# The middle channel block of a convolution, moved from VectorE to ScalarE and accumulating DMAs

## The chip, the cores and the metric

The program runs on one core of a Trainium2 chip. Its engines are TensorE (PE in the profile, its weight loads PEld), VectorE (DVE), ScalarE (ACT), GpSimd (POOL) and SyncE (SP). Each works through its own instructions in the order in which they were written, and waits on semaphores for the others. DMAs are issued from the queues of SP, of POOL and, rarely, of ACT. The metric is the device time of one execution in microseconds (us); less is better.

## The reference

A causal depthwise convolution over 7 positions, whose weights are the softmax of 8 rows (one row for each group of 24 channels), is followed by two matrix products with a gelu between them:

```
w = softmax(weight)                         # (8, 7), row h serves channels 24h .. 24h+23
a[b, s, d] = sum over k of w[h(d), k] * x[b, s - 6 + k, d]      # x is (8, 4096, 192), zeros ahead of it
h = a.reshape(32768, 192) @ w_in            # w_in (192, 2048)
g = h * sigmoid(1.702 * h)
out = g @ w_out                             # w_out (2048, 192), everything float32
```

## The kernel before

**Steps.** The tokens are worked in 32 steps, numbered 0 to 31 (`big` in the code), of 1024 tokens each: two sequences of 512 tokens, side by side. The 192 channels are three blocks of 64 (`c` = 0, 1, 2). One block of a step, with both sequences, is a 128 x 512 tile. The middle block is `c` = 1.

**Two products.** Both matrix products are computed by schemes that save multiplications at the price of additions. The first product of a step (`hidden`, L664, called for v = 0 and v = 1) is 21 terms for each v, each of two 64-row matmuls of 512 columns (`product1`, L611). Its inputs are the convolved blocks and eight sums of them (`SUMS_C`, on GpSimd from step 2 on). The second product (`second`, L973) follows `PLAN` (L926), an order written out by hand. It runs through 78 "go" items: one go is three main matmuls and one side matmul of 128 x 32 by 256 columns. I call the place after n gos "position n". Between the gos, PLAN puts sums of hidden blocks on VectorE (`sum`), accumulating DMAs from GpSimd's queue (`acc`), seeds (ScalarE copies that start an accumulation in PSUM), joins (VectorE additions of partial results) and transposes to the output. A side result is complete every four gos (every two between positions 36 and 42), and ScalarE then copies it out of PSUM (L1016, `act.copy(to, d)`), so that copies stand at positions 4, 8, ..., 36, 38, 40, 42, 46, 50, and so on.

**The blocks of `g`.** The hidden values lie in the tile `g`, in 16 blocks; with four rooms of other tiles they are named "spots" 0 to 20 (spots 5 to 20 are blocks of `g`). A spot has 128 x 1024 values, four quarters of 256. The second product consumes the spots one after the other, so some of them are free again before it is over.

**The convolution before the change.** The convolution of a step is made while earlier steps run, in three ways:

- Block 0: seven ScalarE multiplications (`tap`, L512, the instruction is on L516), one for each k. The first goes to the destination in `conv_t`, the other six to "homes", half-spots of spots 13, 16 and 15. Six accumulating DMAs of 256 KB then add them up in a tree, homes 1+2, 3+4, 5+6, then destination+1, 3+5, destination+3 (`TREE`, L509; `end_taps`, L527, the DMAs are on L530). The taps of step n+2 stand in PLAN of step n, at positions 50, 54, 58, 61, 65, 69 and 72.
- Block 1: one VectorE multiplication and six VectorE multiply-adds (`conv`, L497; L502 and L504), in the first product (v = 0) of the step ahead. `prepare` (L580) lists them, and `work` (L1049) hands them out against a budget of time.
- Block 2: seven ScalarE taps and six GpSimd additions (L518), in the first product (v = 0) of the step ahead, through `taps_at`.

`next_tap` (L1054) emits the next entry of the list `ready`; `need` (L1060) empties a list up to a label.

**What sets the order.** The order on each engine is that of the program text: PLAN in the second product, the calls in `hidden` in the first. The main loop's `begin` puts the preparation of step n+2 into the lists just ahead of the second product of step n.

**The places that matter below.** In PLAN, `("acc", 7, 10)` reads spot 10 and `("acc", 12, 9)` reads spot 9 by a 512 KB DMA; `("acc", 18, 14)` is the last one. At position 58 stand a side copy and then `("seed", "k5", "p2", 1)`, at 60 the join `("join", "p2", "p4", "+", "k3")`, which reads the PSUM region p4 and overwrites p2, whose old value the seed keeps, and at 62 `("main", 4, 6, "p4", 0)`, which accumulates into p4. `("main", 12, 18, "p3", 0)` at 70 reads spot 18.

Of the kernel before, what the change touches and what calls it, by code (L numbers as in the profile page):

```python
# [15 lines left out]
def kernel(  # L16
# [126 lines left out]
        flat = osbs[:, i * BLK : (i + 1) * BLK] if i < 2 else room[:, ROOMS[i - 2], :]  # L143
        return flat.rearrange("p (k t) -> p k t", k=NG)

    KEPT_LATE, TAP_SPOTS = 3, {0: (13, 16, 15), 2: (14, 17, 18), 3: (15, 16, 19)}

    def kept(i):

# [20 lines left out]
    def place(big, b):  # L170

        if b == V1:
            return V8 if big % 2 else C31
        return C31 if b == V8 and big % 2 else b
# [319 lines left out]
    def conv_src(big, c, k, ns=slice(0, 2)):  # L494
        return xts[big][:, c, ns, Q - PAD + k : Q - PAD + k + T]

    def conv(big, c, k, ns=slice(0, 2), times=vec.tensor_scalar_mul):  # L497
        src = conv_src(big, c, k, ns)
        dst = own(big)[:, 2 * c + ns.start : 2 * c + ns.stop, :]
        tap = cw[:, c, k : k + 1]  # L500
        if k == 0:
            times(dst, src, tap)  # L502
        else:
            vec.scalar_tensor_tensor(  # L504
                out=dst, in0=src, scalar=tap, in1=dst, op0=ALU.mult, op1=ALU.add
            )

    DMA_TAPS = (0,)
    TREE = {2: [(1, 2)], 4: [(3, 4)], 6: [(5, 6), (0, 1), (3, 5), (0, 3)]}  # L509
    PAIRS_1 = {2: [(1, 2)], 4: [(3, 4)], 6: [(5, 6)]}  # L510

    def tap(big, c, k):  # L512
# [3 lines left out]
        act.mul(home, conv_src(big, c, k), cw[:, c, k : k + 1])  # L516
        if k and c not in DMA_TAPS and big > 1:
            nc.gpsimd.tensor_add(dst, dst, home)  # L518
# [61 lines left out]
    def prepare(big):  # L580

        v1 = place(big, V1)
        def convs(*cs):
            for c in cs:
                for k in range(K):
                    yield "", 0.76 if k else 0.48, lambda c=c, k=k: conv(big, c, k)

        cost = 0.34 if big == 1 else 0.0
        yield from convs(1)
        yield f"conv {big}", 0.0, lambda: None  # L590
        if big == 1:
            dst = own(1)[:, 0:2, :]
            for k in (1, 3, 5):
                yield "", 0.7, lambda k=k: vec.tensor_add(dst, dst, tap_home(1, 0, k))
        yield f"done {big}", 0.0, lambda: need(f"taps {big}")
        yield "", cost, lambda: sums_c(big, 0)
        yield f"first {big}", 0.0, lambda: cross_when(True, big, v1, v1 + 1)
        yield "", 0.0, lambda: cross_when(False, big, 0, C31)
        for i in range(1, len(SUMS_C)):
            yield "", cost, lambda i=i: sums_c(big, i)  # L600
        rest = (C31, V8) if big % 2 else (C31 + 1, NB)
        yield f"all {big}", 0.0, lambda: cross_when(False, big, *rest)

    def prepare_taps(big):

        for c in (0, 2):
            for k in range(K):
                yield "", 1.0, lambda c=c, k=k: tap(big, c, k)
        yield f"taps {big}", 0.0, lambda: None
# [54 lines left out]
    def hidden(big, v, x, z, y, sums, work, fetch, last=lambda: None):  # L664

        def pe(slot, *ts, first=False):
            terms(big, v, slot, *ts, first=first)

        def taps_at(n):
            for _ in range(0 if v else n):
                next_tap()

        def early(i):
            for item in (EARLY_G if big > 1 else EARLY_G_1)[i] if v else ():
                sum_g(*item)


        if v:  # L680
            pe(z, 7, first=True)
            give(True, big)
        if v:
            pe(sums, 12)
            copy2(k15, sums)
            pe(x, 5, 17)
        else:
            pe(x, 5)
            pe(sums, 12)
            copy2(k15, sums)  # L690
            pe(x, 17)
            taps_at(1)
        gelu(B11, 0, v, x)
        if not v:
            pe(z, 7, first=True)
        pe(sums, 0)
        copy2(k16, sums)
        taps_at(2)
        last()
        def turn_next():  # L700
            if big + 2 < N_BIG:
                need(f"done {big + 1}")
                turn_x(big + 2)

        early(0)
        if not v:
            work(2.0 if big > 1 else 1.6)
        elif big == 1:
            work(3.2)

        pe(y, 6, 14, first=True)
        sum2(vec.tensor_sub, x, z, k15)
        early(1)
        if not v or big == 1:
            work(1.6 if big > 1 else 1.2)
        pe(sums, 13)
        copy2(k19, sums)
        pe(x, 2)
        copy2(k18, x)
        taps_at(2)  # L720
        pe(z, 11)
        pe(sums, 20, 10)
        sum2(vec.tensor_sub, k15, y, k19)
        gelu(B12, 0, v, sums)
        pe(x, 4)
        copy2(k20, x)
        sum2(vec.tensor_sub, k19, z, k19)
        early(2)
        if not v or big == 1:
            work(1.1)  # L730
        gelu(B22, 1, v, k19)
        gelu(B22, 0, v, k15)
        taps_at(2)
        pe(y, 8)
        pe(sums, 1, 9, first=True)
        pe(y, 15)
        if v and big == 1:
            turn_next()
        elif not v:
            work(2.2 if big > 1 else 1.1)  # L740
        sum2(vec.tensor_add, k20, k20, sums)
        sum2(vec.tensor_sub, k16, y, k16)
        gelu(B11, 1, v, k20)
        pe(x, 18)
        gelu(B21, 1, v, x)
        early(3)
        fetch()
        if not v:

            copy2(y, z)  # L750
        gelu(B21, 0, v, k16)
        if not v:
            work(1.2)
        if not v and big > 1:
            turn_next()
        pe(sums, 3, 19)
        if not v:
            work(0.7)
        sum2(vec.tensor_add, k18, k18, sums)
        return lambda: gelu(B12, 1, v, k18)  # L760
# [150 lines left out]
    def store(big, n, o=None, queues=(nc.sync,) * 3):  # L911
# [45 lines left out]
        ("turn", 1, 0, 0, "k6"), ("store", 0, 0), ("main", 24, 19, "p5", 0), ("go", 2), ("final",),  # L957
        ("join", "k1", "p3", "-", "k3"), ("go", 1), ("join", "k2", "p2", "-", "k4"),
        ("turn", 0, 0, 1, "k1"), ("store", 0, 1), ("go", 1), ("turn", 0, 1, 1, "k2"), ("store", 1, 1),
        ("join", "k1", "p5", "+", "k5"), ("turn", 0, 1, 0, "k1"), ("join", "k8", "k8", "+", "k0"),  # L960
        ("turn", 1, 1, 0, "k8"), ("store", 1, 0),
    ]

    def sum_g(dst, a, op, b=None):
# [81 lines left out]

    todo, ready = [], []

    def work(us):  # L1049
        while todo and todo[0][1] <= us + 0.2:  # L1050
            us -= todo[0][1]
            todo.pop(0)[2]()
# [243 lines left out]
```

## Time and profile before

| | us |
|---|---|
| median of 3 runs | 2274.22 (2273.69 to 2274.6) |
| span of the profiled execution, first to last instruction | 2272.6 |
| busy in that span: PE, DVE, ACT, POOL | 2263.4, 1941.0, 1568.8, 847.0 |
| one step in the middle of the span (second product of 17 to that of 18) | 70.06 |

The profiled execution's own total is not listed apart from its span; the span is 1.6 us under the median of the runs, and what lies around it (start and end of the program) is of that size. In a row of groups stand line, engine, operation, output and inputs by tile name, shapes and count, then busy time and the mean of one in ns, then the idle time of the engine ahead of them and what ended it. In a row of the timeline stand start, duration, engine, line, operation, tiles, count, and in brackets an idle time ahead of it with its releaser. A matmul's busy time is no measure of how well PE is used, since matmuls overlap; the regularity of their starts is.

### The profile page before, as it was taken

Reading aid. Unit: us, or ns where it says so; the run is one execution under the profiler, and the core shown is the slowest. Engines: PE = TensorE matmul, PEld = TensorE weight load, DVE = VectorE, ACT = ScalarE, POOL = GpSimd, SP = SyncE. Lnnn points to the kernel's source line nnn. Section 1 sums busy time; section 2 is a strip of 40 time slices with the busy share of each in tenths; the row PEclk is TensorE's granted clock in tenths of the full one; section 3 lists DMA queues with packets and bytes.
Section 4 is the critical chain, followed back from the end, with each engine's and each line's share of the span. In section 5 each row is a group of like instructions: output and inputs, shape, how many; then the busy total and the mean of one; then the engine's idle time right before and its main releaser. Section 6 shows DMA issues by size and latency. Waiting matters only on the chain.

```text
span 2272.6 us, 60950 instructions
## 1 busy us (share of the span) xinstructions
PE 2263.4 (100%) x25214; PEld 1214.9 (53%) x25214; DVE 1941.0 (85%) x2794; ACT 1568.8 (69%) x2972; POOL 847.0 (37%) x834
## 2 busy tenths in 40 slices
PE   9999999999999999999999999999999999999998
PEld 5475555555555555555555555555555555555556
DVE  8998888888888888888888888888888888888877
ACT  8866776667766667666677666776667766667754
POOL 1544443244442344433444324444244442344400
PEclk9999999999999999999999999999999999999999
DMA  9976656656566665666655675656666566664443
GB/s 205 155 146 127 127 111 126 137 122 131 116 126 129 123 139 114 116 126 134 134 120 109 126 144 121 131 112 127 132 126 136 112 124 126 129 139 86 88 99 71
DMA packets 269908, 284.20 MB, mean 125 GB/s; under 512 B 117952, under 2 KB 206016, under 8 KB 269632
## 3 DMA queue, kind: packets, MB, share of 16 engines
q0 software_dynamic: 57648, 150.69, 36.9%
q1 hardware_dynamic: 210336, 129.22, 25.2%
q8 instruction: 199, 3.26, 0.6%
q14 instruction: 77, 0.63, 0.1%
q10 hardware_dynamic: 1648, 0.39, 0.1%
HBM read 53.15 MB, written 25.17 MB: 34 GB/s over the span
## 4 chain that ended last, share of the span: by engine, by line
PE 99%; DVE 1%; ACT 0%; DMA 0%; issue 0%; SPq 0%; ACTq 0%; DVEq 0%
PE slot L616 35%; PE slot L991 33%; PE sums L616 16%; PE sums L991 13%; PE slot L822 2%; DMA xin<-in_x_dram 0%; DVE room L657 0%; DVE xt L473 0%; ACT conv_t L1096 0%; DVE conv_t L504 0%; SPq L99 0%; ACT conv_t L357 0%; DVE room L393 0%; ACT conv_t L356 0%; DVE g L391 0%
## 5 line engine op out<-in xcount | busy, mean ns | idle before, releaser
L616 PE MATMUL slot<-conv_t,w_in_s 64*128 64x512 f32 x3740 | 862.5, 591 | 0.3 <-DVE w_in_s L376 0.3
L991 PE MATMUL slot<-g,w_form 128*32 128x256 f32 x7024 | 710.8, 379 | 0.4 <-DVE room L657 0.4
L616 PEld LDWEIGHTS slot<-conv_t,w_in_s 64*128 64x128 f32 x3740 | 377.6, 187 | 423.9 <-issue 347.7
L393 DVE TENSOR_TENSOR g<-g 128x1024 f32<-128x1024 f32 x372 | 448.9, 1234 | 3.2
L991 PEld LDWEIGHTS slot<-g,w_form 128*32 128x32 f32 x7024 | 375.7, 110 | 118.1 <-DVE room L657 0.9
L616 PE MATMUL sums<-conv_t,w_in_s 64*128 64x512 f32 x1660 | 408.3, 589 | 0.3 <-DVE w_in_s L376 0.3
L1016 ACT COPY room<-slot 32x256 f32<-32x256 f32 x434 | 159.3, 367 | 310.3 <-PE slot L991 309.2
L642 ACT ACTIVATE g<-room 128x1024 f32<-128x1024 f32 x310 | 325.7, 1077 | 67.9 <-DVE room L657 67.9
L991 PE MATMUL sums<-g,w_form 128*32 128x256 f32 x2648 | 368.8, 379 | 0.0
L991 PE MATMUL slot<-g,w_out_s 128*32 128x256 f32 x4080 | 318.8, 380 | 0.0
L967 POOL DMA_DIRECT2D g<-g x124 | 106.2, 857 | 496.6 <-PE slot L991 156.8
L616 PEld LDWEIGHTS sums<-conv_t,w_in_s 64*128 64x128 f32 x1660 | 172.1, 187 | 184.9 <-issue 140.0
L518 POOL TENSOR_TENSOR conv_t<-conv_t,g 128x512 f32<-128x512 f32 x180 | 262.2, 1457 | 16.3 <-POOL conv_t L518 3.0
L530 POOL DMA_DIRECT2D g<-g x120 | 105.5, 879 | 422.5 <-PE sums L991 128.7
L653 ACT COPY room<-slot 128x512 f32<-128x512 f32 x434 | 231.4, 601 | 38.5 <-PE slot L616 38.4
L516 ACT ACTIVATE g<-xt,cw 128x512 f32<-128x512 f32 x360 | 248.5, 730 | 2.2
L991 PEld LDWEIGHTS slot<-g,w_out_s 128*32 128x32 f32 x4080 | 164.7, 110 | 128.5 <-ACT g L638 22.7
L638 ACT ACTIVATE g<-slot 128x512 f32<-128x512 f32 x334 | 180.8, 598 | 45.4 <-PE slot L616 24.8
L991 PEld LDWEIGHTS sums<-g,w_form 128*32 128x32 f32 x2648 | 177.9, 110 | 37.6
L504 DVE SCALAR_TENSOR_TENSOR conv_t<-xt,cw,conv_t 128x512 f32<-128x512 f32 (+1 forms) x198 | 192.0, 970 | 4.6
L393 POOL TENSOR_TENSOR conv_t<-conv_t 128x256 f32<-128x256 f32 x180 | 181.9, 1024 | 9.4
L1016 ACT COPY room<-sums 32x256 f32<-32x256 f32 x217 | 79.6, 367 | 145.0 <-PE sums L991 142.5
(205 smaller groups left out, 2909.5 us busy)
## 6 DMA issues: line engine op xcount, KB each, us to landing
g<-g POOLq DMA_DIRECT2D x124, 512.0 KB, 5.8
xin<-in_x_dram SPq DMA_DIRECT2D x240, 180.0 KB, 4.3
conv_t<-conv_t SPq DMA_DIRECT2D x180, 192.0 KB, 3.1
g<-g POOLq DMA_DIRECT2D x120, 256.0 KB, 3.8
out_dram<-osbs SPq DMA_DIRECT2D x186, 128.0 KB, 4.9
g<-room POOLq DMA_DIRECT2D x31, 512.0 KB, 5.3
conv_t<-g POOLq DMA_DIRECT2D x60, 256.0 KB, 4.8
g<-osbs POOLq DMA_DIRECT2D x30, 512.0 KB, 4.7
```

Of the source, the lines that this page charges most:

```text
L393: eng.tensor_sub(v(dst), v(a), v(b))
L504: vec.scalar_tensor_tensor(out=dst, in0=src, scalar=tap, in1=dst, op0=ALU.mult, op1=ALU.add)
L516: act.mul(home, conv_src(big, c, k), cw[:, c, k : k + 1])
L518: nc.gpsimd.tensor_add(dst, dst, home)
L530: nc.gpsimd.dma_start(out=out, in_=src, accum_op=ALU.add)
L616: nc.tensor.matmul(slot[h], w_in_s[halves[h], a, v * P : (v + 1) * P], src, start=first, stop=True, skip_group_check=True,)
L638: act.activation(dst[:, :, h, :], src[h].rearrange("p (o t) -> p o t", o=2), AF.Gelu_apprx_sigmoid)
L642: act.activation(dst.rearrange("p o h t -> p h o t"), src.rearrange("p h (o t) -> p h o t", o=2), AF.Gelu_apprx_sigmoid,)
L653: act.copy(bank(dst, h), bank(src, h))
L967: nc.gpsimd.dma_start(out=spot(dst), in_=spot(a), accum_op=ALU.add)
L991: nc.tensor.matmul(dst, w, t, start=first, stop=last, skip_group_check=True)
L1016: act.copy(to, d)
```

## The change

For steps 3 to 31, block 1 is made as block 0 is: seven ScalarE taps and six accumulating DMAs, two steps ahead, in PLAN. The homes are half-spots of spots 10, 11 and 9. The seven taps stand in PLAN at positions 36, 38, 40, 42, 44, 47 and 49; the list of a step is now block 1, block 0, block 2, so the seven old places in PLAN still serve block 0, and block 2 stays in the first product. The order of every other entry of PLAN is as before. VectorE's seven instructions of block 1 are gone from these steps, and `work` does nothing for them except in its last call of `hidden`, where the GpSimd sums are emitted; `need("done ...")` in `turn_next` now does the rest. As PLAN belongs to the step two ahead, the second products of steps 1 to 29 have the new work: 29 of them.

```
-    KEPT_LATE, TAP_SPOTS = 3, {0: (13, 16, 15), 2: (14, 17, 18), 3: (15, 16, 19)}
+    KEPT_LATE, TAP_SPOTS = 3, {0: (13, 16, 15), 1: (10, 11, 9), 2: (14, 17, 18), 3: (15, 16, 19)}
...
-    DMA_TAPS = (0,)
+    DMA_TAPS = (0, 1)
...
-        yield from convs(1)
+        if big < 3:
+            yield from convs(1)
...
-        for c in (0, 2):
+        for c in (0, 2) if big < 3 else (1, 0, 2):
...
         if not v:
-            work(2.0 if big > 1 else 1.6)
+            work(2.0 if big > 1 else 1.6, big + 1)
...
-        ("main", 2, 5, "p4", 0), ("go", 1), ("sum", 13, 18, "+", 4), ("go", 2),
-        ("cross",), ("sum", 6, 9, "-", 5), ("go", 1), ("acc", 12, 9), ("main", 20, 0, "p1", 0), ("go", 2),
+        ("main", 2, 5, "p4", 0), ("tap",), ("go", 1), ("sum", 13, 18, "+", 4), ("go", 1), ("tap",), ("go", 1),
+        ("cross",), ("sum", 6, 9, "-", 5), ("go", 1), ("acc", 12, 9), ("main", 20, 0, "p1", 0), ("tap",),
+        ("go", 2), ("join", "k2", "k7", "-", "p4"), ("side", 6, 13, "k8"), ("tap",), ("go", 1),
+        ("join", "k2", "k2", "-", "p2"), ("go", 1), ("sum", 15, 15, "-", 16), ("main", 9, 6, "p4", 0), ("tap",),
+        ("go", 3), ("join", "k9", "p1", "+", "k5"), ("tap",), ("go", 1), ("join", "k10", "p0", "-", "k9"),
+        ("main", 3, 15, "p2", 0), ("go", 1), ("cross",), ("acc", 18, 14), ("tap",), ("go", 1),
...
-    def work(us):
+    def work(us, big=1):
+        if big > 2:
+            return
         while todo and todo[0][1] <= us + 0.2:
```

The other calls of `work` in `hidden` but the last get `big + 1` in the same way.

More of the change, by code (lines that the diff above doesn't have):

```diff
@@ L714, in hidden @@
         if not v or big == 1:
-            work(1.6 if big > 1 else 1.2)
+            work(1.6 if big > 1 else 1.2, big + 1)
         pe(sums, 13)
@@ L729, in hidden @@
         if not v or big == 1:
-            work(1.1)
+            work(1.1, big + 1)
         gelu(B22, 1, v, k19)
@@ L739, in hidden @@
         elif not v:
-            work(2.2 if big > 1 else 1.1)
+            work(2.2 if big > 1 else 1.1, big + 1)
         sum2(vec.tensor_add, k20, k20, sums)
@@ L752, in hidden @@
         if not v:
-            work(1.2)
+            work(1.2, big + 1)
         if not v and big > 1:
@@ L954 @@
         ("join", "k7", "k4", "-", "p4"), ("go", 1), ("tap",), ("join", "k7", "k7", "+", "k3"), ("go", 1),
[2 rows of a table removed]
[2 rows of a table added]
         ("turn", 1, 0, 0, "k6"), ("store", 0, 0), ("main", 24, 19, "p5", 0), ("go", 2), ("final",),
[L958 to L961, printed above, removed]
[3 rows of a table added]
     ]
```

26 rows, old and new, of the table PLAN are left out of this document.

## The prediction

> **What bounds the kernel now.** I read the page first, for which engine bounds and what the chain that ended last is made of.
>
> ```profile
> span 2272.6 us, 60950 instructions
> PE 2263.4 (100%) x25214; PEld 1214.9 (53%) x25214; DVE 1941.0 (85%) x2794; ACT 1568.8 (69%) x2972; POOL 847.0 (37%) x834
> PE 99%; DVE 1%; ACT 0%; DMA 0%; issue 0%; SPq 0%; ACTq 0%; DVEq 0%
> ```
>
> TensorE is busy all the time and is 99% of the chain. Busy time alone does not say that nothing is lost, so the second view is that of stretches: step 1, step 7 and step 17, each from one second product to the next, and the first half (v = 0) of the first product that follows step 17's second one. The columns are length, then PE, PEld, DVE, ACT and POOL, clock, DMA share, GB/s.
>
> ```profile
> 130.43:201.49 71.06, 70.67 (x794) 46.84 (x793) 60.81 (x87) 49.40 (x94) 27.23 (x26) 1.00 0.72 143
> 551.78:622.00 70.22, 70.22 (x795) 36.78 (x793) 60.29 (x85) 48.59 (x93) 27.13 (x26) 1.00 0.64 127
> 1252.68:1322.74 70.06, 70.06 (x794) 36.87 (x792) 60.75 (x85) 48.59 (x93) 27.24 (x26) 1.00 0.63 126
> 1286.40:1304.50 18.10, 18.10 (x88) 8.37 (x86) 15.72 (x24) 15.94 (x28) 9.41 (x8) 1.00 0.55 97
> ```
>
> A step is 70.06 us at full clock. Step 1 is 1.00 us longer, step 7 0.16. So VectorE, with its 60.75 us, costs nothing in a step of 70.06: the removal alone can give back at most what steps 1 and 7 have over a regular one, 1.2 us, or 0.05%. The question is whether the added work makes TensorE late somewhere, 29 times. 0.2% is 4.5 us, or 0.16 us in each of the 29 second products; below that a measurement of this kernel can hardly be told from no change.
>
> **What is removed.** The groups of the four kinds of instructions:
>
> ```profile
> L504 DVE SCALAR_TENSOR_TENSOR conv_t<-xt,cw,conv_t 128x512 f32<-128x512 f32 (+1 forms) x198 | 192.0, 970 | 4.6
> L502 DVE TENSOR_SCALAR conv_t<-xt,cw 128x512 f32<-128x512 f32 (+1 forms) x32 | 14.1, 440 | 0.0
> L516 ACT ACTIVATE g<-xt,cw 128x512 f32<-128x512 f32 x360 | 248.5, 730 | 2.2
> L530 POOL DMA_DIRECT2D g<-g x120 | 105.5, 879 | 422.5 <-PE sums L991 128.7 <-PE slot L991 118.8 <-ACT g L516 87.2
> ```
>
> Six multiply-adds at 970 ns and one multiplication at 440 ns are 6.3 us of VectorE in each step, 182 us over 29. They run in the stretch of the last row above, where VectorE is busy 15.72 of 18.10 us; it will be some 9.4. On the path: 0, since TensorE is busy for the whole 18.10 us beside them, and the ceiling of 1.2 us stands.
>
> **What is added on ScalarE.** Seven taps at 730 ns are 5.1 us in each second product, 148 us in all. They stand between positions 36 and 49, ahead of side copies and of the seed at 58, on an engine that takes its instructions in order. This is the one place where I find little room, so it is worked out, from ScalarE's timeline in step 17 (start, duration):
>
> ```profile
> 1268.50 0.37 ACT L1016 COPY room<-sums 32x256 f32<-32x256 f32 x1 [0.54 <-PE sums L991]
> ...
> 1274.54 0.37 ACT L1016 COPY room<-slot 32x256 f32<-32x256 f32 x1 [1.36 <-PE slot L991]
> 1274.82 0.36 ACT L1020 COPY slot<-room 96x256 f32<-96x256 f32 x1
> 1275.20 0.72 ACT L516 ACTIVATE conv_t<-xt,cw 128x512 f32<-128x512 f32 x1
> 1276.27 0.37 ACT L1016 COPY room<-sums 32x256 f32<-32x256 f32 x1 [0.34 <-PE sums L991]
> 1276.66 0.72 ACT L516 ACTIVATE g<-xt,cw 128x512 f32<-128x512 f32 x1
> 1278.05 0.37 ACT L1016 COPY room<-slot 32x256 f32<-32x256 f32 x1 [0.66 <-PE slot L991]
> 1278.44 0.37 ACT L1020 COPY room<-slot 96x256 f32<-96x256 f32 x1
> 1278.71 1.34 ACT L516 ACTIVATE g<-xt,cw 128x512 f32<-128x512 f32 x2
> 1280.07 0.37 ACT L1016 COPY room<-slot 32x256 f32<-32x256 f32 x1
> ```
>
> The copy at 1268.50 is that of position 36, the one at 1278.05 that of 58; the seed k5 follows at 1278.44. From start to start, back to back: copy to tap 0.39 (1276.27 to 1276.66), copy to seed 0.28, seed to tap 0.38 (1274.54, 1274.82, 1275.20), two taps and on to a copy 1.36 (1278.71 to 1280.07), one tap and on to a copy some 0.73 (its mean time). After the change the row from 36 to 58 is copy, tap 1, copy, tap 2, copy, tap 3, copy, taps 4 and 5, copy, taps 6 and 7, copy, seed, tap 8, copy, tap 9, copy of 58 (taps 8 and 9 are block 0's, there already). With no wait in it that is 6 x 0.39 + 5 x 0.73 + 2 x 1.36 + 0.28 + 0.38 = 9.37 us. From 1268.50 it ends at 1277.87, 0.18 us ahead of 1278.05, when TensorE has the side result ready. So copies in between start up to 0.8 us late, and the backlog is gone at 58.
>
> Who waits for them? The side banks of PSUM are used again only eight or more gos later (3.4 us at 0.43 each, 33.7 us over 78), and the seed into p1 is due at position 60; 0.8 us is covered there. The tight place is behind the seed of 58: a join on VectorE waits for it, and the main of 62 waits for the join. Step 17, then step 7, where a copy happened to be late:
>
> ```profile
> 1278.84 0.43 DVE L391 TENSOR_TENSOR slot<-sums,room 96x256 f32<-96x256 f32 x1 [1.75 <-ACT room L1020]
> 1279.47 0.39 PE L991 MATMUL sums<-g,w_out_s 128*32 128x256 f32 x3
> 577.42 0.37 ACT L1016 COPY room<-slot 32x256 f32<-32x256 f32 x1 [0.94 <-PE slot L991]
> 578.22 0.43 DVE L391 TENSOR_TENSOR slot<-sums,room 96x256 f32<-96x256 f32 x1 [2.03 <-ACT room L1020]
> 578.70 0.42 PE L991 MATMUL sums<-g,w_out_s 128*32 128x256 f32 x3
> ```
>
> Counted from the step's start (1252.68, 551.78), the copy of 58 is at 25.37 and at 25.64, 0.27 later; that step lost 0.16. So 0.12 us of the delay is free and the rest is paid in full. The margin of the new row is 0.18 + 0.12 = 0.30 us.
>
> **Waits inside that row.** Tap 2 writes spot 10 and must wait until the acc of spot 10 has landed, tap 6 likewise for spot 9. The three last accs of step 17, then GpSimd's first and third block-0 DMA; the landing times of all accs of this kind (minimum, median, maximum); the acc of spot 10 in steps 1 and 7, its two latest; the copy of position 36 in step 1:
>
> ```profile
> 1263.90 0.86 POOL L967 DMA_DIRECT2D g<-g  x1 [1.74 <-DVE g L391]
> 1266.17 0.86 POOL L967 DMA_DIRECT2D g<-g  x1 [1.41 <-DVE g L393]
> 1269.67 0.86 POOL L967 DMA_DIRECT2D g<-g  x1 [2.65 <-DVE g L391]
> 1279.72 0.86 POOL L530 DMA_DIRECT2D g<-g  x1 [9.20 <-PE slot L991]
> 1284.46 0.88 POOL L530 DMA_DIRECT2D g<-g  x1 [2.12 <-ACT g L516]
> DMA to landing us min/median/max: 4.5/5.4/8.0
> L967 POOL DMA_DIRECT2D g<-g x1: 858/858/858, 143.0 to 143.0; - x1
> DMA to landing us min/median/max: 7.8/7.8/7.8
> L967 POOL DMA_DIRECT2D g<-g x1: 856/856/856, 563.0 to 563.0; - x1
> DMA to landing us min/median/max: 7.3/7.3/7.3
> 147.22 0.36 ACT L1016 COPY room<-sums 32x256 f32<-32x256 f32 x1 [0.56 <-PE sums L991]
> g<-g POOLq DMA_DIRECT2D x120, 256.0 KB, 3.8
> ```
>
> Tap 2 is reached 0.39 + 0.73 + 0.39 = 1.51 us after the copy of 36, at 1270.01; the acc of 1263.90 lands at 1269.3 by the median. No wait. Tap 6 is reached at 1270.01 + 2 x (0.73 + 0.39) + 1.36 + 0.39 = 1274.00; the acc of 1266.17 lands at 1271.6, by the maximum at 1274.2, inside the margin. In step 1, tap 2 comes at 147.22 + 1.51 = 148.73 and the landing at 143.0 + 7.8 = 150.8: 2.07 late, 1.77 after the margin. In step 7 it comes at 567.60 + 1.51 = 569.11, the landing at 570.3: 1.19 late, 0.89 paid. Bounds: below, both waits hidden, 0; above, the maximum of 8.0 in every step, 1271.9 against 1270.01, 1.59 us x 29 = 46 us. I take the median for 27 steps and the two rows as they are: **+2.7 us**.
>
> The Trainium skill (ScalarE: Activation LUTs, section "What ACT_TABLE_LOAD costs") puts an ACTIVATE with one pointer operand at 280 ns + 0.833 ns per element, 707 ns for 512, with 93 ns of overlap behind another. The rows agree for a tap alone (730) and for two taps, not for a tap ahead of a PSUM copy; by the page's 0.61 the row would be 0.6 us shorter over five single taps, the margin 0.9, and the sum only +1.5 us.
>
> **What is added on GpSimd.** Six DMA issues at 879 ns are 5.3 us a step, and each waits in GpSimd's queue for its tap or for an earlier DMA of the tree. Queued behind them:
>
> - The acc of spot 18. It now stands behind the DMAs of taps 3 and 5. Tap 5 ends at about 1273.6, so it issues at about 1274.2 instead of 1269.67 and lands at 1279.6 by the median, 1282.2 by the maximum. Position 70, which reads spot 18, is at 1252.68 + 70 x 0.43 = 1282.8. Covered, by 0.6 us at worst; 0.
> - Block 0's tree. Block 1's tree starts its third DMA after tap 7, at about 1275.3, and two links of 3.8 us follow: GpSimd is free at about 1283. Block 0's first DMA goes out 3.5 us late, its third still about 1284.5, and its last link waits for that one. Block 2's additions, the eight sums and the crossing DMAs behind them start as before, within about 1 us, and have several us of room in the first product; 0.
>
> SP's queue gets nothing. The added traffic is 6 x 256 KB a step; the DMA engines have a share of 0.63.
>
> **Sum.** 2272.6 + 2.7 = 2275.3 us of span; the median of the runs stands 1.6 above the span, so **2276.9 us** (+0.12%). I count it as no change.
>
> **Rivals.**
>
> - *ScalarE's backlog reaches position 58* (the other side: slower). For it: the margin is only 0.30 us, built of differences of some hundredths, and each tap's wait may cost a little. Against it: all the spacings are read back to back. It decides from 0.07 us a step beyond the margin ((4.5 - 2.7) / 27). Price: at 0.05 us more for each of the 16 links the row is 0.8 us longer, 0.5 beyond the margin; 27 x 0.5 + 2.7 + 2 x 0.8 = 18 us, **2292 us**. At half of that, 2280.
> - *The acc of spot 18 comes late for position 70.* For it: two issues and their waits now stand ahead. Against it: 3.2 us of room by the median. Price at 0.5 us a step: 14.5 + 2.7, **2291 us**.
>   A sentence of the Trainium skill speaks against the change here (SBUF — State Buffer, sections "SBUF: two separate sides" and "Who interferes with whom"): while VectorE runs an instruction in a two-port mode, GpSimd cannot write the descriptors of its DMAs, and a DMA of 620 ns took 3100. By that page two such DMAs ahead of the acc would bring it 5.0 us later, 1.8 us behind position 70 by the median, 52 us in all (an estimate from the page). The rows do not show it: GpSimd's issues take 0.86 us in this part of the step, where VectorE runs additions of two tensors, which the page does not count among the two-port modes; the one instruction of a kind that it does count, L502, is removed.
> - *The waits are hidden altogether*, since landings shift: **2274.2 us**, also no change.
> - *TensorE gains from VectorE's freedom.* Against it: the regular 70.06. At most 1.2 us, 2273.0; not 0.2%.
>
> **How the numbers follow.** My forecast (with the hidden-waits case) 0.62; backlog 0.28; spot 18 and anything else that stalls TensorE 0.08; a gain over 0.2% 0.02. So faster 0.02, same 0.62, slower 0.36. The range reaches from 2273.4 (nothing lost, step 7's stall gone) to 2288, which leaves out the worse half of the backlog case.
>
> **What would show it.** In the profile after: DVE's busy time some 180 us less, ACT's some 148 more, POOL's 150 more, a step still 70.06; the copy of 58 at 25.37 of its step; the extra idle time in front of TensorE only at position 62 of steps 1 and 7. Wrong would be a step that is regularly longer, with the join at 60 waiting for ScalarE (backlog), a start after 1282.8 for position 70 (spot 18), or a stall in the first product, which I hold to be untouched.

## The result, and the profile after

The changed kernel takes 2337.82 us (median of four runs, 2331.67 to 2340.03) against 2274.22 us (2273.69 to 2274.6): the ratio is 1.0276, with a 95% interval of 1.0261 to 1.0291. It is 63.6 us slower, and the predicted 2276.9 us and its range up to 2288 do not hold it.

The profiled execution took 2340.03 us, with a span of 2338.3 us. From the page of the changed kernel: span, busy times of the engines, and the chain that ended last by engine.

```profile
span 2338.3 us, 61557 instructions
PE 2284.0 (98%) x25214; PEld 1227.3 (52%) x25214; DVE 1804.8 (77%) x2591; ACT 1697.7 (73%) x3175; POOL 1011.3 (43%) x1008
PE 61%; POOL 15%; DMA 12%; DVE 5%; issue 4%; ACT 3%; SPq 0%; POOLq 0%; DVEq 0%; ACTq 0%
```

VectorE fell by 136 us, ScalarE rose by 129, GpSimd by 164. The chain was 99% TensorE; now 15% of it is GpSimd and 12% are transfers, more than half of that the one transfer `g<-osbs` (7%). Lines of the code from some L611 on have moved by one or not at all, so L616, L642, L653 and L657 of before are L617, L643, L654 and L658 here, and L967, L991, L1016 and L1020 are the same.

The groups of instructions that changed their idle time, first in the kernel before, then in the changed one. The columns are busy time and mean ns of one, then the idle time of the engine just before them and what ended it.

```profile
L393 DVE TENSOR_TENSOR g<-g 128x1024 f32<-128x1024 f32 x372 | 448.9, 1234 | 3.2
L991 PE MATMUL slot<-g,w_out_s 128*32 128x256 f32 x4080 | 318.8, 380 | 0.0
L991 PE MATMUL sums<-g,w_out_s 128*32 128x256 f32 x1872 | 148.5, 379 | 0.0
```

```profile
L393 DVE TENSOR_TENSOR g<-g 128x1024 f32<-128x1024 f32 x372 | 458.9, 1254 | 79.5 <-DMA g<-osbs 76.3
L991 PE MATMUL slot<-g,w_out_s 128*32 128x256 f32 x4080 | 325.0, 385 | 29.1 <-DVE g L393 28.7 <-DVE slot L391 0.4
L991 PE MATMUL sums<-g,w_out_s 128*32 128x256 f32 x1872 | 148.9, 380 | 16.4 <-DVE g L393 16.0 <-DVE slot L391 0.4
```

This is the place of the loss. VectorE's sums waited 76.3 us for one transfer, `g<-osbs`, and TensorE 28.7 + 16.0 = 44.7 us for those sums, of 65.7 us by which the span grew; TensorE's busy time is 20.6 us longer, in part by a slower clock behind the longest of these waits (last section). `g<-osbs` occurs once in a step: it is the item (8, 0, "acc") of EARLY_G (L922), the accumulating DMA that adds spot 0 to spot 8 late in the first product. VectorE's `("sum", 7, 8, "-", 7)` at position 6 reads spot 8, the sums behind it wait in line, and `("main", 5, 8, "p1", 0)` at position 16 waits for `("sum", 8, 8, "-", 16)`. Of the 30 steps from step 1 on, the median is 71.76 us long instead of 70.06, and in 27 TensorE sits idle for 0.34 to 4.88 us from 7.1 us of the second product on, at position 16.

Why the transfer is late is seen in GpSimd's queue, here its timeline from step 17 on, to the next `g<-osbs`. First before (the second product starts at 1252.68), then after (it starts at 1284.59).

```profile
1295.55 0.86 POOL L530 DMA_DIRECT2D conv_t<-g  x1 [6.27 <-issue]
1296.12 9.05 POOL L518 TENSOR_TENSOR conv_t<-conv_t,g 128x512 f32<-128x512 f32 x6
...
1317.56 0.87 POOL L967 DMA_DIRECT2D g<-osbs  x1 [3.47 <-issue]
```

```profile
1308.67 1.13 POOL L530 DMA_DIRECT2D g<-g  x1
1310.47 0.86 POOL L530 DMA_DIRECT2D conv_t<-g  x1 [0.68 <-DMA g<-g]
1315.75 0.86 POOL L530 DMA_DIRECT2D g<-g  x1 [4.42 <-issue]
1320.20 0.86 POOL L530 DMA_DIRECT2D conv_t<-g  x1 [3.60 <-DMA g<-g]
1320.74 2.97 POOL L530 DMA_DIRECT2D g<-g  x3
1327.39 0.86 POOL L530 DMA_DIRECT2D conv_t<-g  x1 [3.68 <-DMA g<-g]
1331.23 0.86 POOL L530 DMA_DIRECT2D g<-g  x1 [2.99 <-DMA g<-g]
1335.22 0.86 POOL L530 DMA_DIRECT2D conv_t<-g  x1 [3.13 <-DMA g<-g]
1335.78 10.09 POOL L518 TENSOR_TENSOR conv_t<-conv_t,g 128x512 f32<-128x512 f32 x6
...
1353.64 0.87 POOL L967 DMA_DIRECT2D g<-osbs  x1
```

The second fence begins with the third DMA of block 1's tree and its last three links, each of which waits for the landing of earlier ones (0.68, 4.42 and 3.60 us of idle time; the profile names no releaser for the 4.42, but the third DMA takes 6.6 us to land, from 1308.67 to 1315.3, and the link follows at 1315.75). Block 0's three first DMAs, taken from 27.04 us of the step on in the kernel before, all go out at 36.15 (1320.74 - 1284.59), and their own links follow one landing after the other. Block 2's additions begin at 51.19 instead of 43.44, and the transfer for spot 8 goes out at 69.05 instead of 64.88, with no idle time ahead of it where there were 3.47 us before.

What that does to VectorE at the start of step 17: the landing of the transfer that belongs to it and VectorE's timeline, before and after.

```profile
L967 POOL DMA_DIRECT2D g<-osbs x1: 873/873/873, 1247.6 to 1247.6; - x1
DMA to landing us min/median/max: 5.0/5.0/5.0
1253.99 4.63 DVE L393 TENSOR_TENSOR g<-g 128x1024 f32<-128x1024 f32 x4
```

```profile
L967 POOL DMA_DIRECT2D g<-osbs x1: 850/850/850, 1282.7 to 1282.7; - x1
DMA to landing us min/median/max: 6.3/6.3/6.3
1288.99 4.75 DVE L393 TENSOR_TENSOR g<-g 128x1024 f32<-128x1024 f32 x4 [2.02 <-DMA g<-osbs]
1292.54 0.42 PE L991 MATMUL slot<-g,w_out_s 128*32 128x256 f32 x3 [0.83 <-DVE g L393]
```

Before, the transfer lands 0.1 us ahead of the second product, and the second of VectorE's four sums, the one at position 6, starts 2.4 us into it. After, it lands 4.4 us into it, VectorE starts that sum 2.0 us late, and TensorE idles 0.83 us. The rest of step 17 runs behind this stall, so that the step is 1.04 us longer. The next transfer is late because the trees stand in the queue again, and not because a delay is handed on: step 1 has no such stall and step 2 has one of 3.17 us, and behind the 3.77 us of step 13 stand 0.51 in step 14.

### The profile page after: what moved, and what is told of

It is laid out like the page before. It is cut to its first block, busy times and chain, and to the rows that moved or that the text cites. A ratio compares the mean times of both kernels' runs of the same rounds, so it can differ in the third digit from the quotient of the medians.

```text
span 2338.3 us, 61557 instructions
## 1 busy us (share of the span) xinstructions
PE 2284.0 (98%) x25214; PEld 1227.3 (52%) x25214; DVE 1804.8 (77%) x2591; ACT 1697.7 (73%) x3175; POOL 1011.3 (43%) x1008
## 4 chain that ended last, share of the span: by engine, by line
PE 61%; POOL 15%; DMA 12%; DVE 5%; issue 4%; ACT 3%; SPq 0%; POOLq 0%; DVEq 0%; ACTq 0%
PE slot L991 24%; PE slot L617 18%; PE sums L991 10%; PE sums L617 7%; DMA g<-osbs 7%; POOL conv_t L518 6%; POOL conv_t L393 6%; DMA g<-g 4%; DVE g L393 3%; POOL conv_t L391 2%; PE slot L823 2%; DMA xin<-in_x_dram 1%; DVE room L658 1%; ACT g L516 1%; ACT g L639 1%
## 5 line engine op out<-in xcount | busy, mean ns | idle before, releaser
L617 PE MATMUL slot<-conv_t,w_in_s 64*128 64x512 f32 x3740 | 865.2, 591 | 0.6 <-DVE room L658 0.4
L991 PE MATMUL slot<-g,w_form 128*32 128x256 f32 x7024 | 711.7, 379 | 0.9 <-DVE room L658 0.4
L617 PEld LDWEIGHTS slot<-conv_t,w_in_s 64*128 64x128 f32 x3740 | 389.0, 187 | 414.2 <-issue 333.0
L393 DVE TENSOR_TENSOR g<-g 128x1024 f32<-128x1024 f32 x372 | 458.9, 1254 | 79.5 <-DMA g<-osbs 76.3
L991 PEld LDWEIGHTS slot<-g,w_form 128*32 128x32 f32 x7024 | 372.7, 110 | 122.5 <-ACT slot L1020 1.3
L617 PE MATMUL sums<-conv_t,w_in_s 64*128 64x512 f32 x1660 | 410.7, 590 | 0.3 <-DVE w_in_s L376 0.3
L530 POOL DMA_DIRECT2D g<-g x236 | 223.5, 1137 | 416.0 <-DMA g<-g 168.2
L516 ACT ACTIVATE g<-xt,cw 128x512 f32<-128x512 f32 x534 | 368.0, 726 | 19.7 <-DMA g<-g 15.7
L643 ACT ACTIVATE g<-room 128x1024 f32<-128x1024 f32 x310 | 325.7, 1077 | 68.8 <-DVE room L658 68.7
L991 PE MATMUL sums<-g,w_form 128*32 128x256 f32 x2648 | 369.1, 379 | 0.1
L991 PE MATMUL slot<-g,w_out_s 128*32 128x256 f32 x4080 | 325.0, 385 | 29.1 <-DVE g L393 28.7
L1016 ACT COPY room<-slot 32x256 f32<-32x256 f32 x434 | 158.1, 364 | 243.1 <-PE slot L991 240.4
L518 POOL TENSOR_TENSOR conv_t<-conv_t,g 128x512 f32<-128x512 f32 x180 | 298.7, 1659 | 11.8
L617 PEld LDWEIGHTS sums<-conv_t,w_in_s 64*128 64x128 f32 x1660 | 178.1, 187 | 180.4 <-issue 137.2
L654 ACT COPY room<-slot 128x512 f32<-128x512 f32 x434 | 231.5, 601 | 38.5 <-PE slot L617 38.4
L991 PEld LDWEIGHTS slot<-g,w_out_s 128*32 128x32 f32 x4080 | 164.3, 111 | 164.1 <-DVE g L393 35.3
L530 POOL DMA_DIRECT2D conv_t<-g x118 | 114.5, 970 | 313.6 <-DMA g<-g 239.7
L967 POOL DMA_DIRECT2D g<-g x124 | 116.1, 936 | 304.5 <-PE slot L991 92.5
L991 PEld LDWEIGHTS sums<-g,w_form 128*32 128x32 f32 x2648 | 177.1, 110 | 38.2 <-ACT sums L1020 1.0
L658 DVE TENSOR_TENSOR room<-slot,room 128x512 f32<-128x512 f32 x248 | 156.0, 679 | 35.4 <-ACT room L654 35.4
L393 POOL TENSOR_TENSOR conv_t<-conv_t 128x256 f32<-128x256 f32 x180 | 175.6, 990 | 9.2
```

The costliest lines, as they stand in the source:

```text
L393: eng.tensor_sub(v(dst), v(a), v(b))
L530: nc.gpsimd.dma_start(out=out, in_=src, accum_op=ALU.add)
L617: nc.tensor.matmul(slot[h], w_in_s[halves[h], a, v * P : (v + 1) * P], src, start=first, stop=True, skip_group_check=True,)
L643: act.activation(dst.rearrange("p o h t -> p h o t"), src.rearrange("p h (o t) -> p h o t", o=2), AF.Gelu_apprx_sigmoid,)
L654: act.copy(bank(dst, h), bank(src, h))
L658: op(*(bank(t, h) for t in (dst, a, b)))
```

## The experiments

Three theories stood at the start. **Queue**: block 1's dependent links hold GpSimd's queue, and everything behind them comes late, up to the transfer for spot 8. **Traffic**: 1.5 MB more in each step slow every transfer, wherever it stands. **ScalarE**: the taps hold ScalarE's row, the prediction's first rival. The times of the kernel before that the runs were compared with are 2274.11 us for the first four runs, 2274.25 for the next four and 2273.77 for the last three.

**e2_no_links, taps without transfers.** The taps of block 1 are made and never added up. In `tap`, for the changed kernel:

```diff
+        if c == 1:
+            return
         homes = [dst] + [tap_home(big, c, i) for i in range(1, K)]
```

> The changed kernel, ScalarE's seven taps of block 1 kept, but without the six accumulating transfers that add them up (block 1 of the conv is then tap 0 alone). Queue theory (GpSimd's queue, held by block 1's dependent links, sends the sum for spot 8 too late) and traffic theory (1.5 MB more per step lengthen every transfer): both causes are gone, 2274 to 2278, the prediction's own +2.7 us for ScalarE waiting on spots 10 and 9 being all that is left. ScalarE theory (its row of copies up to position 58 comes late): nothing changes, 2330 to 2340.

2275.11 us, ratio 1.0004 (0.9995 to 1.0014). With all taps of the changed kernel on ScalarE the loss is gone, so the ScalarE theory falls. The taps' group in this run:

```profile
L516 ACT ACTIVATE g<-xt,cw 128x512 f32<-128x512 f32 x534 | 368.0, 726 | 7.2 <-DMA g<-g 3.3
```

Waiting for accs costs these taps 3.3 us in all on ScalarE, and of TensorE's steps only step 1 and step 23 are longer than before (71.41 against 71.06 us, 70.21 against 70.06).

**e3_spread, the same transfers in another order.** The last three links of block 1 are kept back and sent one by one behind links of block 0:

```diff
-        for a, b in (PAIRS_1 if big == 1 and c == 0 else TREE).get(k, ()):
+        pairs = (PAIRS_1 if big == 1 and c == 0 else TREE).get(k, ())
+        if c == 1 and k == K - 1:
+            held.extend((homes[a], homes[b]) for a, b in pairs[1:])
+            pairs = pairs[:1]
+        for i, (a, b) in enumerate(pairs):
             tree.append((homes[a], homes[b]))
+            if held and c == 0 and i in (0, 2):
+                tree.append(held.pop(0))
...
```

> The changed kernel with the same six transfers of block 1, only in another order in GpSimd's queue: the last three links, which each wait for an earlier landing, are sent one at a time behind block 0's first, second and third link. Queue theory: block 0's tree starts some 9 us earlier, GpSimd's additions and sums go back to within 2 us of before, the transfer for spot 8 lands before VectorE's sum at position 6, and the time falls to 2274 to 2290. Traffic theory: as many bytes at the same part of the step, 2325 to 2340. ScalarE theory: 2330 to 2340.

2275.39 us, ratio 1.0005 (0.9995 to 1.0014). Nothing but the order in one queue differs from the changed kernel, and 62 of its 63.6 us are gone. GpSimd's timeline of step 17 (start 1252.73; the lines of this part of the code have moved on by six), then rows of the DMA issues (KB each, us to landing), the changed kernel's first:

```profile
1274.26 1.20 POOL L973 DMA_DIRECT2D g<-g  x1
...
1279.77 0.86 POOL L536 DMA_DIRECT2D g<-g  x1 [3.42 <-PE slot L997]
...
1298.48 8.39 POOL L518 TENSOR_TENSOR conv_t<-conv_t,g 128x512 f32<-128x512 f32 x6
...
1317.66 0.87 POOL L973 DMA_DIRECT2D g<-osbs  x1 [2.11 <-DVE osbs L391]
```

```profile
g<-g POOLq DMA_DIRECT2D x236, 256.0 KB, 5.3
```

```profile
g<-g POOLq DMA_DIRECT2D x236, 256.0 KB, 5.2
```

Block 0's first DMA goes out at 27.04 us of the step as before, block 2's additions start at 45.75, and the transfer for spot 8 goes out at 64.93, after waiting 2.11 us for its own operand. The traffic theory falls with this run too: the transfers are as many, and the 256 KB ones take 5.2 us to land, as in the changed kernel (3.8 before), yet no time is lost by it.

**e4_sum_vector, spot 8 without GpSimd.** The accumulating DMA becomes a sum on VectorE:

```diff
-        ..., [(0, 5, "+", 6), (8, 0, "acc")], [(2, 9, "-", 0)],
+        ..., [(0, 5, "+", 6)], [(8, 8, "+", 0), (2, 9, "-", 0)],
```

> The changed kernel, except that the sum for spot 8 (spot 8 plus spot 0) is one VectorE instruction of about 1.25 us in the first product in place of GpSimd's accumulating transfer at the end of its queue. Queue theory: nothing that TensorE needs early hangs on GpSimd's queue any more, the stall at position 16 goes, 2274 to 2282. Traffic theory: the other accumulating transfers of the second product are as slow as before and VectorE's sums behind them too, 2310 to 2340. ScalarE theory: 2330 to 2340.

2282.3 us, ratio 1.0037 (1.0024 to 1.005), just past the upper end of what the queue theory expected (2282). Block 1's links still stand ahead of block 0's here, and GpSimd's additions of block 2 still begin late (1306.60 in the step that starts at 1255.92, 50.68 us into it), but nothing that TensorE needs early hangs on them: 55 of the 63.6 us are gone. So the loss reaches TensorE through this one transfer. The 8.2 us that remain were the question of the last run.

**e11_sum_vector_before.** The same edit in the kernel before.

> The kernel before with the sum for spot 8 on VectorE in place of GpSimd's accumulating transfer, nothing else. It says what the 8 us are that the changed kernel still lost with the sum on VectorE. If they come from VectorE, which has one sum of 1.2 us more ahead of the second product: 2278 to 2283 here too, or more, since VectorE still has its seven multiply-adds. If they come from the trees: 2274 to 2275 here.

2278.66 us, ratio 1.0022 (1.0013 to 1.0031): 4.9 of the 8 us come with the sum on VectorE alone, without trees of block 1. Nearly every step is 70.19 us here, 0.13 longer than before. The other 3 us, in single steps of the run with block 1's trees (step 24 is 71.23 us, step 29 71.15; in both TensorE waits some 0.5 us for a VectorE addition at the start of the second product), were not followed further.

**e6_pool_4, e9_pool_6, e10_pool_8, e7_pool_12, GpSimd delayed by itself.** In the kernel before, in `prepare`, n sums more (4, 6, 8 or 12):

```diff
         for i in range(1, len(SUMS_C)):
             yield "", cost, lambda i=i: sums_c(big, i)
+        for _ in range(n if big > 2 else 0):
+            yield "", cost, lambda: sums_c(big, len(SUMS_C) - 1)
```

> The kernel before; from step 3 on GpSimd computes the last of its eight sums four times more (same operands, same result), no transfer is added, ScalarE and VectorE are left alone. One such sum takes 0.73 to 1.7 us, so the transfer for spot 8 stands 2.9 to 6.8 us later in the queue. It waits 3.47 us for its own operand in the kernel before and lands 2.56 us ahead of VectorE's sum at position 6: room for 6.0 us. Queue theory: 2274 to 2276. If GpSimd's queue has no such room, some us per step, 2300 and above. Traffic theory: nothing changes, 2274.

> As the run with four more sums, with twelve: 8.8 us later at 0.73 us each, up to 20 us at 1.7. Queue theory: past the 6.0 us of room by 2.8 us or more, the stall at position 16 appears in every step as in the changed kernel, with no taps on ScalarE and no byte more in transfers: above 2310. Traffic and ScalarE theories: nothing changes, 2274 to 2276.

2273.88 us with four (ratio 0.9998, 0.9988 to 1.0007) and 2525.26 us with twelve (1.1097, 1.1081 to 1.1114). From these two a size could be forecast:

> As the runs with four and twelve more sums on GpSimd, with six. With four the transfer for spot 8 landed 0.96 us into the second product, 1.48 us ahead of VectorE's sum at position 6; in the changed kernel that sum started 1.96 us late and TensorE stalled 1.0 to 1.2 us for it, so TensorE has some 0.8 us of room more. A sum more took 1.03 us on average in the run with twelve. Queue theory: two more are 2.1 us, VectorE's sum 0.6 us late, TensorE just not: 2274 to 2277. Traffic theory: 2274.

> With eight more sums, four more than the run with four: 4.1 us later, 1.48 + 0.8 = 2.3 us of it covered. Queue theory: TensorE loses about 1.8 us in each of some 28 steps, 2274 + 50 = 2324, within 2300 to 2345, and the stall stands at position 16. Traffic theory: 2274.

2276.38 us with six (1.0014, 1.0005 to 1.0024; in the profiled execution the stall stands in one step, 1.81 us in step 16), and 2324.64 us with eight (1.0217, 1.0199 to 1.0234), against the 2274 to 2277 and the 2324 forecast. Nothing is added on ScalarE in these runs, no byte of traffic and no link of a tree, and the profile of the changed kernel comes back: VectorE and TensorE of one step with twelve (start 1386.33; lines moved on by two), and GpSimd's row ahead of the transfer.

```profile
1394.49 4.75 DVE L393 TENSOR_TENSOR g<-g 128x1024 f32<-128x1024 f32 x4 [5.05 <-DMA g<-osbs]
1398.04 0.65 PE L993 MATMUL slot<-g,w_out_s 128*32 128x256 f32 x3 [4.59 <-DVE g L393]
...
1449.88 17.39 POOL L393 TENSOR_TENSOR conv_t<-conv_t 128x256 f32<-128x256 f32 x16
1467.21 0.86 POOL L969 DMA_DIRECT2D g<-osbs  x1
```

The same two waits are there, 5.05 us instead of 2.02 on VectorE and 4.59 instead of 0.83 on TensorE. The room in GpSimd's queue is thus known from both sides: four sums of about 1 us fit into it, six nearly do (2.6 us lost in the whole run), and past that the delay is paid in every step.

**e8_tap_58, the margin on ScalarE.** In PLAN, on top of the spread links:

```diff
-        ("go", 2), ("seed", "k5", "p2", 1), ("tap",), ("cross",),
+        ("go", 2), ("tap",), ("seed", "k5", "p2", 1), ("cross",),
```

> The run with block 1's dependent links spread, with one tap moved ahead of ScalarE's copy at position 58 instead of behind it. The prediction read 0.30 us of margin for that copy before TensorE's position 62 waits; the tap takes 0.61 us of the row, so 0.31 us are lost in each of 28 steps: 2275.4 + 8.7 = 2284. If the copy has more room than was read, 2275; if the copy's delay is passed on whole, 2275.4 + 17 = 2292.

2289.5 us, ratio 1.0066 (1.005 to 1.0083). This tap ends up behind the copy of position 58 and ahead of the seed, which is a ScalarE copy too. The join that waits for the seed, and the main of position 62, with spread links (step starts at 1252.73) and then with the tap moved (1261.68):

```profile
1278.88 0.43 DVE L391 TENSOR_TENSOR slot<-sums,room 96x256 f32<-96x256 f32 x1 [1.71 <-ACT room L1026]
1279.51 0.39 PE L997 MATMUL sums<-g,w_out_s 128*32 128x256 f32 x3
```

```profile
1288.46 0.43 DVE L391 TENSOR_TENSOR slot<-sums,room 96x256 f32<-96x256 f32 x1 [2.32 <-ACT room L1026]
1288.95 0.42 PE L997 MATMUL sums<-g,w_out_s 128*32 128x256 f32 x3 [0.30 <-DVE slot L391]
```

The join comes at 26.78 us instead of 26.15, the main at 27.27 instead of 26.78: of 0.63 us, 0.49 are paid. The steps are 70.56 us long instead of 70.06, and 29 x 0.50 = 14.5 us is about the difference of the two runs (2289.5 - 2275.4 = 14.1). The expectation used the whole margin of 0.30, but 0.18 of it lie ahead of the copy, and this tap stands behind it. The 0.12 us that the prediction read behind the copy is what was found (0.63 - 0.50 = 0.13).

**e1_no_conv and e5_no_conv_held, the removal alone.** Both leave block 1 of the convolution uncomputed from step 3 on: they are the kernel before with `yield from convs(1)` under `if big < 3:`; the second also has the changed kernel's hold on `work`.

> The kernel before, without the seven VectorE instructions of block 1 from step 3 on (block 1 of the conv is not computed there; nothing takes its place). The prediction priced this removal at 0 to -1.2 us, because TensorE's own 70.06 us set a step: 2273.0 to 2274.2. If VectorE had been a bound anywhere in the step, the time falls below 2270.

2324.99 us, ratio 1.0223 (1.0208 to 1.0238), where a gain of 1.2 us at most was expected. ScalarE at the start of the first product behind step 17's second one, and the first TensorE row behind it:

```profile
1319.49 3.79 ACT L516 ACTIVATE g<-xt,cw 128x512 f32<-128x512 f32 x6
1323.18 2.03 ACT L654 COPY room<-slot 128x512 f32<-128x512 f32 x4
1323.80 1.18 PE L617 MATMUL slot<-conv_t,w_in_s 64*128 64x512 f32 x3 [1.01 <-ACT room L654]
```

Six taps of block 2 stand in a row ahead of four copies that TensorE waits for; the kernel before has two there. Without the seven items of the conv, the list that `work` hands out reaches at once the item that calls for all taps of the step. The run missed its expectation because it measured another order on ScalarE, so it was repeated with the order held.

> The kernel before, without the seven VectorE instructions of block 1 from step 3 on (block 1 is not computed there), and with the changed kernel's hold on the list of due work, so that everything else is sent in the order of the kernel before: the removal alone. The prediction's price for it: 0 to -1.2 us, 2273.0 to 2274.2. If what made the run without the conv slow is the removal itself and not ScalarE's taps sent earlier, about 2325 again.

2274.43 us, ratio 0.9999 (0.999 to 1.0009). VectorE's busy time falls from 1941.0 to 1773.8 us, and nothing that can be measured changes.

## Why the prediction was wrong, by its own steps

- **What bounds the kernel**, and "What is removed ... On the path: 0": right. With the removal alone the time stays the same (e5), a step at 70.06 us. VectorE's 136 us less in the changed kernel, for some 180, and ScalarE's 129 us more, for some 148, were sizes off without effect on the time.
- **"What is added on ScalarE"**: right. In the changed kernel the copy of position 58 in step 17 starts at 26.41 us of the step (1311.00), 25.37 plus the 1.04 us that TensorE's stall had cost earlier in that step; with spread links it is at 25.37 exactly (1278.09).

```profile
1311.00 0.37 ACT L1016 COPY room<-slot 32x256 f32<-32x256 f32 x1
```

```profile
1278.09 0.37 ACT L1022 COPY room<-slot 32x256 f32<-32x256 f32 x1 [0.63 <-PE slot L997]
```

- **"Waits inside that row", +2.7 us**: right in kind. The taps alone cost 2275.11 - 2274.11 = 1.0 us, between -1.1 and 3.2 by the interval. The two steps that it priced at 1.77 and 0.89 us lost 0.35 (step 1, 71.41 against 71.06) and nothing (step 7, 70.06); 0.15 fell to step 23.
- **"The acc of spot 18 ... Covered"**: right. With spread links it goes out at 21.53 us of the step (1274.26), as worked out, and lands at 27.44, ahead of position 70 at 30.1. The rule of the Trainium skill that the prediction set against it (SBUF — State Buffer, section "Who interferes with whom") did not show: by it two issues would have brought the DMA 5.0 us later (the prediction's estimate), and it came at the time worked out without it. This is no disagreement, since VectorE ran additions of two tensors there, as the prediction had said.
- **"Block 0's tree ... start as before, within about 1 us, and have several us of room in the first product; 0"**: this is the step that failed, in three numbers. The links of block 1 were priced at 3.8 us each, the median of a kernel in which fewer of them were in flight. In the changed kernel the median is 5.3 us; in step 17 the two landings that hold the queue took 6.6 and 3.9 us, the third DMA of block 1 went out at 24.08 us of the step and not at 22.6 (1275.3), and GpSimd was free for block 0 at 36.15 and not at 30.3 (1283). (By its own figures, 1283 - 1279.72, block 0 would have been 3.3 us late, not the 3.5 written.) Then "its third still about 1284.5, and its last link waits for that one" held only if that tree were bound by taps; with all three of its first DMAs sent at once and late, its links came one landing after the other, and the last was issued at 50.63 (1335.22) instead of 42.87 (1295.55). And the "several us of room" were not worked out from a row. For the transfer from step 17 to 18, the landings before and after:

```profile
L967 POOL DMA_DIRECT2D g<-osbs x1: 873/873/873, 1317.6 to 1317.6; - x1
DMA to landing us min/median/max: 5.4/5.4/5.4
```

```profile
L967 POOL DMA_DIRECT2D g<-osbs x1: 868/868/868, 1353.6 to 1353.6; - x1
DMA to landing us min/median/max: 7.1/7.1/7.1
```

  The room is 3.47 us of idle time ahead of the transfer (its row above: 1317.56), 2.2 us between its landing and VectorE's sum, 2.4 us into step 18, and some 0.95 behind that until TensorE waits (in step 17 after, the sum is 1.96 us late and TensorE's matmuls of position 16 are 1.01): 6.6 us in all. Against it stand additions that came 7.75 us late, 1.04 of them by the step's own stall, so 6.7, and a transfer that took 1.7 us longer to land: 8.4. The 1.8 us that are left are about what step 18 lost (1.51 us of idle time; its matmuls of position 16 are 1.68 us late).
- **The rivals**: none of the four occurred. The list of what would be wrong named "a stall in the first product" and looked for the damage there; it came one second product later, at position 16, because what ends GpSimd's queue in one step is the first thing that VectorE needs in the next.

Open is why the stall differs so much from step to step (none in step 15, 4.88 us in step 29). Issue and landing add up: the transfer for step 15 goes out 2.74 us ahead of that step and takes 6.2 us to land, the one for step 29 goes out 0.72 us into it and takes 7.7. With sums alone the stall varies too (4.6 to 8.0 us with twelve). Why the chain in the queue and the landings vary was not settled; no run held them fixed.

## What to carry to other kernels

When work moves into a queue that runs in order, cost not only its instructions but the longest chain of waits in it, and follow everything queued behind to its last entry, across the end of the loop's body: the room that decides may belong to the next step. Before calling that room ample, add up its parts from rows, the idle time ahead of the last entry and the time from its landing to its reader. If dependent links must share a queue, place independent ones between them; here that order alone was worth 62 us.

## What the runs showed of the hardware that was not expected

A long stall costs TensorE a second time. TensorE's stalls in three steps of the changed kernel, with the stretches behind the first two (length, PE, PEld, DVE, ACT, POOL, clock, DMA share, GB/s):

```profile
1006.80 0.42 PE L991 MATMUL slot<-g,w_out_s 128*32 128x256 f32 x3 [3.77 <-DVE g L393]
861.94 0.42 PE L991 MATMUL slot<-g,w_out_s 128*32 128x256 f32 x3 [3.48 <-DVE g L393]
1579.55 0.42 PE L991 MATMUL slot<-g,w_out_s 128*32 128x256 f32 x3 [3.34 <-DVE g L393]
1007.30:1010.55 3.25, 3.25 (x36) 1.70 (x32) 3.25 (x4) 0.36 (x1) 0.86 (x1) 0.50 0.03 5
862.40:865.50 3.10, 3.10 (x64) 1.90 (x60) 3.10 (x4) 0.37 (x1) 0.86 (x1) 1.00 0.01 1
```

After 3.77 us of idle time the granted clock is 0.50 for the next 3 us, and 36 matmuls run in 3.25 us, against 64 in 3.10 us at full clock. A slow clock also follows the stall of 3.34 us and those of three more steps (3.43, 3.97 and 4.88 us), but not that of 3.48 us. The price is seen in the length of the steps: 75.37 us with the stall of 3.34 us, 73.86 with that of 3.48. The Trainium skill (TensorE: Matmul & The Clock Gate, section "What's actually happening") says that one idle window of about 3.4 us halves the clock until a window has been busy, and that the windows run free of the program. The trace agrees, the 3.34 and the 3.48 us included, which a fixed threshold could not give; where the windows lie it does not show. With twelve more sums on GpSimd, where TensorE idles more than 4 us in every step from step 2 to step 30, the mean granted clock of the run is 0.959: of the 251 us lost there, 181 are idle time in front of the second product's matmuls, by these two groups, and TensorE's busy time is 72.0 us longer than in the kernel before (2335.4 against 2263.4), for which the slow clock is the likely cause.

```profile
L993 PE MATMUL slot<-g,w_out_s 128*32 128x256 f32 x4080 | 342.6, 400 | 84.0 <-DVE g L393 84.0
L993 PE MATMUL sums<-g,w_out_s 128*32 128x256 f32 x1872 | 173.8, 427 | 97.0 <-DVE g L393 97.0
```
